# Two stages of the first expert put back to back, and its w1/w2 products in plain float32

## The chip, the cores and the metric

The kernel runs on one core of a Trainium2 chip. The core has five engines with a queue of instructions each: TensorE (PE; its weight loads are listed as PEld), VectorE (DVE), ScalarE (ACT), GpSimd (POOL) and SyncE (SP), which issues transfers. They run beside each other and wait for one another by semaphores. The metric is the time of one execution on the device in microseconds (us); the median of three runs is compared.

## The reference, cut to what matters

Three things follow one another: attention with a threshold per row, a router that sends each of 2304 tokens to one of eight experts with 288 places each, and a gated network that is the same for all tokens.

```python
scores = np.matmul(q, k.transpose(0, 1, 3, 2)) / np.sqrt(64)      # 4 x 8 heads, 576 x 576
thresh = scores.max(axis=-1, keepdims=True) - tau
x = softmax(np.where(scores >= thresh, scores, -1e9)) @ v          # -> 2304 x 512

order = np.argsort(-(x @ w_gate_router).flatten())                 # 2304 x 8 logits, best first
for idx in order:                                                  # greedy, at most 288 per expert
    tok, e = idx // 8, idx % 8
    if assigned[tok] < 0 and counts[e] < 288:
        assigned[tok] = e; counts[e] += 1

for e in range(8):                                                 # 512 -> 1024 -> 512
    y[assigned == e] = np.maximum(x[assigned == e] @ w1[e], 0) @ w2[e]

gate = 1 / (1 + np.exp(-(y @ w_gate)))                             # 512 -> 1536
out = (gate * (y @ w_val)) @ w_out                                 # 1536 -> 512
```

## The kernel before, in words

**Attention** takes the first part of the span, up to about 390 us, with its orders written out by hand in tables. It leaves the tokens `xd` in device memory and the logits.

**The router** (`Router`, lines 593 to 899) works in eight rounds. Each round searches a threshold, by counting on VectorE and small products on TensorE (line 682: up to 18 passes with 8 columns; line 700: one pass that carries the found bits to all partitions), picks one expert with its 288 tokens and writes their numbers as `idx` (TensorE: lines 830 to 832 and the 18 passes of line 864). The first rounds use `search`, those from `WIDE` = 3 on `search_wide`, which reloads tiles `kw`. A round's first steps need nothing of the expert products. Its expert is done in the order in which the rounds find it, so "first expert" is that of round 0.

**The expert part** has two stages per expert. The tokens of one expert are the 288 columns of every product.

- `arrive(e)`: POOL gathers the tokens by `idx` (three transfers), TensorE turns them (line 1183, twelve transposes in four groups), ScalarE writes the high part `xh` and VectorE the low part `xl` of the turned tokens.
- `stage_m(e)`, the w1/w2 stage: eight products `m1` with pieces of w1 and eight products `m2` with pieces of w2. All products with weights are made of parts: a float32 matrix w is split into a high part and a remainder, both in the format fp32r, and so is x, and one product is `wh*xh + wl*xh + wh*xl`, four passes of each, twelve in all (`thrice`, line 1139, and `onto`, line 1149). A pair of pieces comes as one tile `wr` of 512 KB (line 1211); ScalarE makes the high part (line 1220), VectorE the remainder with `minus` (line 1047), into the tiles `w0` and `w1`. Between `m1` and `m2` the result is passed through relu and split into `hh` and `hl`. After the eighth `m2`, ScalarE and VectorE write the sums out of four accumulators as `yh` and `yl` (line 1134).
- `stage_g(e)`, the gate/val/out stage: twelve times a gate product, a val product and, one step behind, an out product of the gated values `gh` and `gl`. Then the results are turned back into rows (line 1351), copied as `orow` (line 1358) and scattered by POOL.

The weights of gate, val and out are the same for all experts: 36 pieces. Thirteen of them are made ready during attention. The other 23 come as packed tiles `wd` of 512 KB (line 1071) and cost VectorE three narrowing steps (lines 1080 to 1086) and a `minus` each during the first experts. The out weights are stored in parts (`wod`) and loaded again as `wo` for every later expert.

**What sets the order.** `Plan` (from line 922) builds the order of all queues when the kernel is built. Every piece of work is a job with an engine, an estimated duration, the jobs it needs, a priority (a lower number goes first) and the buffers (`Hold`) it takes or uses: among them 3 tiles `wr`, 2 `w0`, 2 `w1`, 3 PSUM tiles for products and nine large tiles shared by `xh`, `xl`, `yh`, `yl`, `wd` and `kw`. `step` always places the job that can start first by the estimates. On TensorE the expert products form a row of their own, the main row: first the jobs that are ready "late enough" (by their `lag`, from `PATIENT`: 15 for the transposes, 30 for the rows), then the main row, then the rest. `open_stage` says which stage comes next in the main row. There is one special arrangement: the first two steps of the first expert's gate/val/out stage (four products) stand ahead of the second expert's w1/w2 stage, and the rest behind it. Between the last attention work and the first product, `warm` (line 1468) puts `PB` = 7 products that nobody uses.

```python
m_seq[1] = g_seq[0][:4] + m_seq[1]
g_seq[0] = g_seq[0][4:]
```

## Time and profile before

| | |
|---|---|
| median of three runs | 1159.14 us (1158.89 to 1161.96) |
| profiled execution, its own time | 1159.21 us |
| its span on the core | 1157.4 us |
| mean granted TensorE clock | 0.966 |
| TensorE busy | 92% of the span, 7938 matmul records |
| VectorE busy | 72%, 2015 instructions |
| ScalarE, GpSimd busy | 45%, 28% |

The span runs from the first to the last recorded event; 1.8 us of the execution's time lie around it. The line `PEclk` of the profile cuts the span in 40 slices of 29 us: the digit is the mean clock that TensorE was granted, in tenths of full speed. TensorE knows two levels, 1.2 and 2.4 GHz, so a clock of 0.5 in a stretch means that all of it ran at the lower one. The first product of the first expert starts at 406.4 us. The share of busy time of an engine is an average over stages that differ; the tables by stretch below tell them apart. A row of the order of time gives start, duration, engine, line, output from inputs and count, and in brackets how long the engine had stood before and what ended the wait. A row of a group gives the number of instructions, then their busy time in all and the mean duration of one in ns, then the idle time ahead of them.

### The profile page before, as it was taken

The page shows a single profiled execution, that of the slowest core. Times are in us where ns is not written, and L with a number is a line of the kernel's source. Part 1 is how long each engine was busy: PE and PEld are TensorE (multiplying, and loading weights), DVE is VectorE, ACT ScalarE, POOL GpSimd, SP SyncE. Part 2 cuts the span into 40 slices and gives each one's busy share as a digit, 9 for nine tenths or more (in the row PEclk, how much of TensorE's full clock was granted, in tenths as well). Part 3 has the DMA queues.
Part 4 walks back from the last instruction along what each step waited for, and adds up shares of the span by engine and source line. Part 5 has one row for each costly group of instructions (what it writes and reads, how often), then busy time and mean ns, then how long its engine had stood idle before and what let it go on. Part 6 is the DMA issues. An engine that isn't in the chain of part 4 may idle for free.

```text
span 1157.4 us, 21194 instructions
## 1 busy us (share of the span) xinstructions
PE 1063.9 (92%) x7938; PEld 994.1 (86%) x7938; DVE 837.1 (72%) x2015; ACT 526.2 (45%) x1120; POOL 323.0 (28%) x334
## 2 busy tenths in 40 slices
PE   4899998999995398999999999999999999999997
PEld 3787877878784297999999899999999999999996
DVE  7999999999997888988587786975973412412411
ACT  4788887788873333533214313413413413413411
POOL 6788888788841100001002001100100100000001
PEclk9999999999997597999999999999999999999998
DMA  7322423323104654454635536435544434433232
GB/s 278 141 84 94 143 84 116 121 84 131 51 18 162 210 182 166 174 191 175 194 110 163 154 107 188 148 106 161 166 118 142 151 110 132 144 110 117 71 110 92
DMA packets 52887, 156.20 MB, mean 135 GB/s; under 512 B 11568, under 2 KB 16560, under 8 KB 50864
## 3 DMA queue, kind: packets, MB, share of 16 engines
q1 hardware_dynamic: 49712, 145.40, 38.6%
q0 software_dynamic: 3072, 9.44, 2.8%
q8 instruction: 63, 1.03, 0.4%
q14 instruction: 40, 0.33, 0.1%
HBM read 135.38 MB, written 19.43 MB: 134 GB/s over the span
## 4 chain that ended last, share of the span: by engine, by line
PE 34%; DVE 30%; issue 25%; DMA 6%; ACT 2%; POOL 1%; SPq 1%; DVEq 0%; POOLq 0%; ACTq 0%
PE ps L1139 15%; PE acc L1149 9%; DVE p L281 6%; DVE nm L259 6%; PE s L248 4%; DVE big L763 3%; DVE th L267 2%; DVE lo L346 2%; PE t L289 1%; DMA kw<-kx 1%; DMA wf<-wf 1%; PE o L373 1%; PE o L365 1%; DVE w L1047 1%; POOL out L1362 1%
## 5 line engine op out<-in xcount | busy, mean ns | idle before, releaser
L1307 DVE TENSOR_TENSOR gt<-ps,sg 128x288 f32<-128x288 f32 x96 | 43.7, 455 | 146.3 <-PE ps L1139 137.2
L1362 POOL DMA_INDIRECT out<-orow,idx x24 | 23.8, 990 | 409.2 <-ACT orow L1358 406.8
L1149 PE MATMUL acc<-gh,wo 128*128 128x288 f32 x768 | 124.0, 298 | 6.0 <-DMA wo<-wod 3.0
L1303 ACT ACTIVATE sg<-ps 128x288 f32<-128x288 f32 x96 | 39.5, 411 | 196.0 <-PE ps L1139 155.3
L263 ACT ACTIVATE e<-s,nm 128x576 f32<-128x576 f32 x144 | 104.9, 741 | 37.8 <-DVE nm L259 35.5
L1047 DVE TENSOR_TENSOR w<-wr,w 128x512 fp32r<-128x512 f32 x128 | 86.3, 689 | 49.2 <-ACT w L1220 48.3
L1220 ACT ACTIVATE w<-wr 128x512 fp32r<-128x512 f32 x128 | 79.1, 629 | 90.5 <-PE acc L1149 38.3
L1311 ACT ACTIVATE gh<-gt 128x288 fp32r<-128x288 f32 x96 | 42.6, 444 | 161.4 <-DVE gt L1307 159.0
L1149 PEld LDWEIGHTS acc<-gh,wo 128*128 128x128 f32 x768 | 108.0, 188 | 7.8 <-issue 2.6
L248 PE MATMUL s<-kh,qs 128*128 128x288 f32 x320 | 80.2, 333 | 34.1 <-DVE p L281 23.4
L1139 PE MATMUL ps<-yh,wgh 128*128 128x288 f32 x384 | 108.5, 304 | 3.3 <-ACT orow L1358 2.1
L1164 POOL DMA_INDIRECT xr<-xd,idx x16 | 15.4, 960 | 337.0 <-issue 155.8
L259 DVE TENSOR_REDUCE nm<-s 128x1 f32<-128x576 f32 x144 | 104.1, 748 | 4.5 <-PE s L248 3.7
L1139 PE MATMUL ps<-yh,wvh 128*128 128x288 f32 x384 | 106.9, 300 | 0.0
L1139 PE MATMUL ps<-yh,wgl 128*128 128x288 f32 x384 | 106.7, 299 | 0.0
L1139 PE MATMUL ps<-yh,wvl 128*128 128x288 f32 x384 | 105.4, 297 | 0.0
L281 DVE SCALAR_TENSOR_TENSOR p<-s,th,e 128x576 f32<-128x576 f32 x128 | 100.1, 808 | 4.3 <-ACT tf L319 0.5
L248 PEld LDWEIGHTS s<-kh,qs 128*128 128x128 f32 x320 | 52.5, 196 | 55.2 <-issue 35.0
L1149 PE MATMUL acc<-hh,w 128*128 128x288 f32 x512 | 84.3, 299 | 0.9 <-ACT ot L1341 0.9
L1139 PE MATMUL ps<-xh,w 128*128 128x288 f32 x512 | 82.5, 304 | 0.6 <-DVE w L1047 0.3
L289 PE MATMUL t<-idf,p 128*128 128x128 f32 x548 | 80.1, 279 | 0.9 <-ACT lo L344 0.7
L763 DVE TENSOR_SCALAR_CACHE_REDUCE big<-kw,tw 128x1152 bf16<-128x1152 f32 x56 | 79.1, 1412 | 1.8
(229 smaller groups left out, 2775.0 us busy)
## 6 DMA issues: line engine op xcount, KB each, us to landing
wo<-wod SPq DMA_DIRECT2D x84, 512.0 KB
wr<-in_w SPq DMA_DIRECT2D x64, 512.0 KB
qkr<-in_qk SPq DMA_DIRECT2D x15, 1248.0 KB
wd<-in_w SPq DMA_DIRECT2D x36, 512.0 KB
wod<-wo SPq DMA_DIRECT2D x12, 512.0 KB
vr<-in_v SPq DMA_DIRECT2D x16, 320.0 KB
kw<-kx SPq DMA_DIRECT2D x64, 72.0 KB
xd<-xl SPq DMA_DIRECT2D x8, 512.0 KB
```

The costliest lines, as they stand in the source:

```text
L248: nc.tensor.matmul(s[:, h, 0:288], qs[:, qo : qo + 128], kt[:, ko + 288 * h : ko + 288 * h + 288], start=m == 0, stop=m == len(src) - 1,)
L259: nc.vector.tensor_reduce(d[u]["nm", i], d[u]["s", i][:, :, 0:288], op=OP.max, axis=AX.XY, negate=True)
L263: nc.scalar.activation(e, d[u]["s", i][:, :, 0:288], AF.Exp, bias=d[u]["nm", i])
L281: nc.vector.scalar_tensor_tensor(dst.rearrange("p (c n) -> p c n", c=2), w["s", i][:, :, 0:288], nmth[n // 2][1][:, n % 2 : n % 2 + 1], w[ ...
L289: nc.tensor.matmul(t[:m, 128 * j : 128 * j + 128], src, idf, is_transpose=True, start=j == 0, stop=j == len(srcs) - 1, skip_group_check=True,)
L763: v.tensor_scalar(self.big, self.kw[h], thr, None, op0=OP.is_ge, op1=OP.add, accum_out=cnt[:, h : h + 1])
L1047: V.tensor_sub(l, x, h.bitcast(F32))
L1139: nc.tensor.matmul(ps, w(q), x[:, q], start=n == 0, stop=n == 11)
L1149: nc.tensor.matmul(acc[m][:, :CAP], w[:, 128 * m : 128 * m + 128], x, start=first and i == 0, stop=last and i == 2)
L1220: A.activation(box[nm][:, 0], box["r"][:, i], AF.Copy)
L1307: V.tensor_tensor(box["gt"], box["v"][:, :CAP], box["sg"], op=OP.mult)
L1311: A.activation(box["h"][0], box["gt"], AF.Copy)
```

## The change

Seven things are changed, all in the plan and in the jobs of the expert part.

1. The products of the first expert's w1/w2 stage are plain float32 matmuls: four passes of 128 rows each, written once, from `wr` as it was loaded and from unsplit `xh` and `hh`. Its splits (ScalarE's high parts and VectorE's remainders, 16 of each), `xl` and `hl` fall away, and so do `w0` and `w1` for this expert; a tile `wr` is held until both its products are done.
2. The special arrangement of the main row goes. The first expert's gate/val/out stage stands whole behind its w1/w2 stage, then come the second expert's two stages.
3. What follows a product (`hh`, `hl`, the sigmoid, the gated value and its parts) gets a priority 40 below that of the stage (`NEAR`) instead of 1, `yh` and `yl` likewise; `yh` are kept in sequence, and so are the results of the out products.
4. The transposes' `PATIENT` goes from 15 to 2; those of the first expert and the rows of the last get priority -2 instead of -1, and two jobs of TensorE at -1 are kept 1.7 us apart by the estimates (`SPACE`).
5. The router's round 1 gets priority 0 instead of -5.
6. `warm` makes 18 products instead of 7.
7. Some estimates of the plan: a gather 3.8 us and 589824 bytes, SP's start at 5.5, a plain product 2.12.

Lines behind the top of the expert part move down: 1139 becomes 1144, 1149 becomes 1154, 1183 becomes 1188, 1211 becomes 1216. The plain products stand in lines 1239 (w1) and 1262 (w2).

```diff
...
+        self.free["SP"] = START
...
-                can = [(r, j) for r, j in can if r + j.lag <= self.free[e]] + main + [(r, j) for r, j in can if r + j.lag > self.free[e]]
+                late = [(r, j) for r, j in can if (r + j.lag if j.prio != -1 else max(r + j.lag, self.spaced)) <= self.free[e]]
+                can = late + main + [x for x in can if x not in late]
...
+            if j.prio == -1:
+                self.spaced = t + SPACE
...
-        hx = {e: [Hold(big), Hold(big)] for e in range(8)}
+        hx = {e: [Hold(big) for i in range(2 if e else 1)] for e in range(8)}
...
-                return 196608
+                return 589824
...
-            gathered = gather_job[e] = job("POOL", 3.2, gather, (), None, acq=hr)
+            gathered = gather_job[e] = job("POOL", 3.8, gather, (), None, acq=hr)
...
-                a = first = job("PE", 0.27, tr, [gathered] if q == 0 else [gathered, first], -1, acq=[hp_] + (hx[e] if q == 0 else []), use=hr + (hx[e] if q else []), lag=PATIENT[0] if e else 0.0)
+                a = first = job("PE", 0.27, tr, [gathered] if q == 0 else [gathered, first], -1 if e else -2, acq=[hp_] + (hx[e] if q == 0 else []), use=hr + (hx[e] if q else []), lag=PATIENT[0] if e else 0.0)
                 b = job("ACT", 0.32, evh, [a], pr, use=[hp_] + hx[e])
-                last.append(job("DVE", 0.39, evl, [b], pr, use=[hp_] + hx[e]))
+                last.append(job("DVE", 0.39, evl, [b], pr, use=[hp_] + hx[e]) if e else b)
...
-                    a = job("ACT", 0.56, hi, [ld], pr, acq=[hd], use=[hr])
-                    half.append(job("DVE", 0.64, lo, [a], pr, use=[hd, hr]))
+                    if e:
+                        a = job("ACT", 0.56, hi, [ld], pr, acq=[hd], use=[hr])
+                        half[i] = job("DVE", 0.64, lo, [a], pr, use=[hd, hr])
...
+                    if e == 0:
+                        for q in range(4):
+                            nc.tensor.matmul(
+                                box["ps"][:, :CAP], box["r"][:, 0, 128 * q : 128 * q + 128], X[0][0][:, q], start=q == 0, stop=q == 3
+                            )
+                        return
...
+                    if e == 0:
+                        for m in range(4):
+                            nc.tensor.matmul(
+                                accs["a"][m][:, :CAP], box["r"][:, 1, 128 * m : 128 * m + 128], box["h"][0], start=j == 0, stop=j == 7
+                            )
+                        return
...
-                a = job("PE", 1.59, m1, [half[0]] + x_dep, None, acq=[hps], use=[h0] + hx[e])
-                b = job("ACT", 0.32, evh, [a], base - 1, acq=[hh], use=[hps])
-                b = job("DVE", 0.39, evl, [b], base - 1, use=[hps, hh])
-                c = job("PE", 1.59, m2, [b, half[1]], None, acq=[hacc] if j == 0 else [], use=[h1, hh] + ([hacc] if j else []))
+                own = [h0] if e else [hr]
+                a = job("PE", 1.59 if e else 2.12, m1, [half[0]] + x_dep, None, acq=[hps], use=own + hx[e])
+                b = job("ACT", 0.32, evh, [a], base - NEAR, acq=[hh], use=[hps])
+                if e:
+                    b = job("DVE", 0.39, evl, [b], base - NEAR, use=[hps, hh])
+                own = [h1] if e else [hr]
+                c = job("PE", 1.59 if e else 2.12, m2, [b, half[1]], None, acq=[hacc] if j == 0 else [], use=own + [hh] + ([hacc] if j else []))
...
-                pr = pos_m[e] + 15
+                pr = pos_m[e] + 16 - NEAR
...
+                a.order = yhi[:1]
...
-                s = job("ACT", 0.31, sig, [a], base - 1, acq=[hsg], use=[hpg])
+                s = job("ACT", 0.31, sig, [a], base - NEAR, acq=[hsg], use=[hpg])
...
+                od[-1].order = od[:1] if m else []
...
-        m_seq[1] = g_seq[0][:4] + m_seq[1]
-        g_seq[0] = g_seq[0][4:]
...
-            if m < 8 and (m == g or m - g < 2 and (m == 1 or xl_jobs[m][-1].end is not None and all(d.end is not None for j in m_seq[m][:2] for d in j.deps))):
+            if m < 8 and (m == g or m - g < 2 and xl_jobs[m][-1].end is not None and all(d.end is not None for j in m_seq[m][:2] for d in j.deps)):
...
-                        job("PE", 2.5, warm, [prev], -1, acq=[Hold(pw)])
+                        job("PE", 5.5, warm, [prev], -1, acq=[Hold(pw)])
...
-            j = job(eng, dur, fn, deps, -1000 if r == 0 else -5 if r == 1 else pos_m[r] - (12 if r == 2 else AHEAD), acq=acq, use=use)
+            j = job(eng, dur, fn, deps, -1000 if r == 0 else 0 if r == 1 else pos_m[r] - (12 if r == 2 else AHEAD), acq=acq, use=use)
...
-PATIENT = 15.0, 30.0
-WD, NWF, LEAD, LATE, PB, WIDE, AHEAD = 4, 3, 14, 3, 7, 3, 40
+NEAR = 40
+PATIENT = 2.0, 30.0
+START, SPACE = 5.5, 1.7
+WD, NWF, LEAD, LATE, PB, WIDE, AHEAD = 4, 3, 14, 3, 18, 3, 40
...
```

How the order of the instructions moves, at three places. Numbers behind an underscore in a name are those of a buffer.

TensorE, the end of the first expert's w1/w2 stage. `hh` and `hl` are the parts behind relu, line 830 to 832 and 864 the last steps of round 1, `yh`/`wgh`/`wgl` the first gate product. Before:

```order
L1149 MATMUL acc<-hh,w_5871 128x288 x2
L1149 MATMUL acc<-hl,w_5871 128x288
L830 LDWEIGHTS tri
L830 MATMUL rps<-s,tri 128x1
...
L832 LDWEIGHTS one
L832 MATMUL rps<-s,one 128x1
L864 LDWEIGHTS oh_5998
L864 MATMUL rps<-rh,oh_5998 96x6
...
L864 MATMUL rps<-rh,big 96x6
L1139 MATMUL ps<-yh,wgh 128x288
```

After:

```order
L1262 MATMUL acc<-hh,wr 128x288 x4
L830 LDWEIGHTS tri
L830 MATMUL rps<-s,tri 128x1
...
L832 MATMUL rps<-s,one 128x1
L1262 MATMUL acc<-hh,wr 128x288 x4
L1144 MATMUL ps<-yh,wgh 128x288
...
L1144 MATMUL ps<-yl,wvh 128x288 x4
L864 LDWEIGHTS oh_5875
L864 MATMUL rps<-rh,oh_5875 96x6
```

Line 864 of round 1 moves from ahead of the first gate product to behind the first val product, and the count of lines 830 to 832 to ahead of the last product of w2.

TensorE, the transposes of the second expert (`idf` is the unit matrix, `xr` and `xs` the gathered rows). Before:

```order
L1139 MATMUL ps<-yl,wvh 128x288 x4
L1183 MATMUL ps<-idf,xr 128x96 x2
L1183 MATMUL ps<-idf,xs 128x96
...
L1139 MATMUL ps<-xh,w_6006 128x288 x8
L1139 MATMUL ps<-xl,w_6006 128x288 x4
```

After:

```order
L1144 MATMUL ps<-yl,wvh 128x288 x4
L700 LDWEIGHTS one
L700 MATMUL rps<-fl,one 128x8
L1188 MATMUL ps<-idf,xr 128x96 x2
L1188 MATMUL ps<-idf,xs 128x96
...
L1154 MATMUL acc<-gh,wo 128x288 x8
L1154 MATMUL acc<-gl,wo 128x288 x4
L1144 MATMUL ps<-yh,wgh 128x288
```

All four groups stood behind the second val product of the first expert and directly ahead of the second expert's first product. Now three of them stand in the middle of the first expert's gate/val/out stage; the fourth stands at that stage's end, ahead of the second expert's first product.

SP, the loads during the first expert's w1/w2 stage, with the semaphores that each waits for (`wr` is a tile of w1 and w2, `wd` a packed piece of the gate, val or out weights). Before:

```order
L1211 ISA
L1211 DMA wr<-in_w 128x1024 [waits DMAHW6_49,DMAHW2_49,DVE_49]
L1211 ISA
L1211 DMA wr<-in_w 128x1024 [waits DMAHW7_49,DMAHW3_49,DVE_49]
L1071 DMA wd<-in_w 128x1024 [waits DMASW1_49,DMASW0_49,PE_49]
L1211 ISA
L1211 DMA wr<-in_w 128x1024 [waits DMAHW0_49,DVE_49]
```

After:

```order
L1216 ISA
L1216 DMA wr<-in_w 128x1024 [waits DMAHW2_49,PE_49]
L1076 DMA wd<-in_w 128x1024 [waits DMAHW3_49,DMASW1_49,DMASW0_49]
L1076 DMA wd<-in_w 128x1024 [waits DMAHW4_49,DMASW2_49]
L1216 ISA
L1216 DMA wr<-in_w 128x1024 [waits DMAHW5_49,PE_49]
L1076 DMA wd<-in_w 128x1024 [waits DMAHW6_49]
L1076 DMA wd<-in_w 128x1024 [waits DMAHW7_49]
```

A load of `wr` waited for VectorE, the last to read the tile; now it waits for TensorE, and two loads of `wd` stand between two of `wr`.

## Rows read from the trace of the kernel before

**Rows 1.** The page: busy time of each engine, and TensorE's clock in 40 slices.

```profile
PE 1063.9 (92%) x7938; PEld 994.1 (86%) x7938; DVE 837.1 (72%) x2015; ACT 526.2 (45%) x1120; POOL 323.0 (28%) x334
...
PEclk9999999999997597999999999999999999999998
```

**Rows 2.** Busy time by stretch: us, busy time per engine, clock, DMA share, GB/s.

```profile
404.00:410.50 6.50, 6.24 (x42) 5.71 (x41) 5.75 (x16) 1.99 (x6) 0.00 (x0) 0.50 0.49 165
410.50:439.20 28.70, 28.70 (x273) 26.79 (x273) 25.49 (x75) 12.45 (x26) 0.00 (x0) 1.00 0.41 146
442.00:448.50 6.50, 5.99 (x36) 5.82 (x37) 5.76 (x18) 3.05 (x5) 1.02 (x2) 0.53 0.78 284
455.00:462.00 7.00, 6.53 (x29) 5.97 (x30) 5.64 (x12) 3.53 (x8) 0.00 (x0) 0.51 0.45 163
489.00:493.00 4.00, 4.00 (x20) 3.71 (x19) 3.26 (x9) 0.48 (x1) 0.00 (x0) 0.57 0.40 135
1004.50:1008.00 3.50, 3.50 (x17) 3.50 (x16) 0.12 (x1) 0.41 (x1) 0.76 (x2) 0.51 0.44 155
493.00:610.00 117.00, 114.63 (x928) 111.10 (x927) 89.02 (x235) 31.34 (x69) 5.56 (x9) 1.00 0.52 167
610.00:1000.00 390.00, 381.64 (x2936) 375.17 (x2935) 249.46 (x653) 126.67 (x284) 30.31 (x45) 1.00 0.47 144
```

**Rows 3.** TensorE's order of time around the first expert, 397 to 458.

```profile
397.66 3.02 PE L1468 MATMUL ps<-big,tri 128*128 128x512 bf16 x7
...
406.44 2.26 PE L1139 MATMUL ps<-xh,w 128*128 128x288 f32 x8 [0.26 <-PE rps L700]
...
442.46 1.31 PE L864 MATMUL rps<-rh,oh 128*96 128x6 bf16 x12 [3.04 <-DVE rh L857]
...
455.37 0.42 PE L1183 MATMUL ps<-idf,xr 96*128 96x96 f32 x1 [1.70 <-DMA xr<-xd,idx]
...
457.75 2.29 PE L1139 MATMUL ps<-xh,w 128*128 128x288 f32 x8
```

**Rows 4.** TensorE: a group by line and form, then the order of time.

```profile
L389 PE MATMUL o<-r,ot 128*128 128x72 f32 x248 | 31.8, 272 | 0.1
...
44.44 1.01 PE L389 MATMUL o<-r,ot 128*128 128x72 f32 x8
45.29 0.60 PE L289 MATMUL t<-idf,pt 128*128 128x128 f32 x4
...
82.02 1.03 PE L289 MATMUL t<-idf,p 128*128 128x128 f32 x8
82.81 0.47 PE L361 MATMUL o<-hi,vh 128*128 128x512 f32 x1
...
1131.48 0.30 PE L1139 MATMUL ps<-yh,wgh 128*128 128x288 f32 x1
...
1136.21 0.30 PE L1139 MATMUL ps<-yh,wgh 128*128 128x288 f32 x1
```

**Rows 5.** Groups by line: whole span; line 682 from 406.5 to 439.

```profile
L1047 DVE TENSOR_TENSOR w<-wr,w 128x512 fp32r<-128x512 f32 x128 | 86.3, 689 | 49.2 <-ACT w L1220 48.3
...
L1134 DVE TENSOR_TENSOR yl<-acc,yh 128x288 fp32r<-128x288 f32 x32 | 12.5, 450 | 1.5 <-ACT yh L1128 1.5
...
L682 PE MATMUL rps<-C,big 128*31 128x8 bf16 x54 | 1.8, 167 | 0.0
```

**Rows 6.** The order of time: a load of `wr` issued, and its first use.

```profile
469.85 0.34 SPq L1211 DMA_DIRECT2D wr<-in_w  x1
...
473.25 0.63 ACT L1220 ACTIVATE w<-wr 128x512 fp32r<-128x512 f32 x1 [0.22 <-DMA wr<-in_w]
```

**Rows 7.** TensorE's order of time: waits behind the first expert.

```profile
487.17 2.02 PE L1149 MATMUL acc<-gh,wo 128*128 128x288 f32 x8 [0.98 <-DVE yl L1134]
...
571.68 1.30 PE L1149 MATMUL acc<-gh,wo 128*128 128x288 f32 x8 [1.59 <-DMA wo<-wod]
...
1004.03 0.40 PE L1139 MATMUL ps<-yh,wgh 128*128 128x288 f32 x1 [2.06 <-ACT orow L1358]
```

## What the change does to the time: the prediction

> **What bounds the kernel now.** I read the page first: TensorE is busy for 92% of the span, VectorE for 72%, and the granted clock is at full level nearly everywhere behind the attention part [rows 1]. From 400 us on TensorE is the engine that everything waits for, so a change is worth what it does to TensorE's own work, to the gaps in its row and to its clock. The table by stretch shows where that is lost [rows 2]: from 410.5 to 439.2 it is busy without a gap at full clock, and VectorE beside it for 25.5 of 28.7 us; four short stretches (from 404, 442, 455 and 489 us) have a granted clock of 0.50 to 0.57, which is the lower of its two levels (1.2 of 2.4 GHz) for most of each. The order of time on TensorE gives the reasons [rows 3]. It stands for 3.04 us up to 442.46 for VectorE's `rh`, and then for gathered rows of the second expert, 1.70 us up to 455.37 alone, until that expert's first product starts at 457.75. Each time it stands or does little first, and then the clock is found at half. So between 439.3 and 457.8, 18.5 us, it does four products, one router step and one set of transposes.
>
> **The products without parts.** At full clock three products of split parts take 1136.21 less 1131.48, 4.73 us, or 1.58 each, 0.131 for each of twelve passes [rows 4]. Sixteen of them go: 25.2 us. In their place stand 64 plain float32 products of 288 columns. The trace has no such product. The plain float32 products of line 389 show that one is executed as two records, each with a load: 248 records (8 more stand under another name) for 16 times 8 products. Lower bound: each record at the price of a split pass, 0.26 us a product, 17 us in all, a gain of 8. Upper bound: eight records of 72 columns at line 389 take 0.85 us (44.44 to 45.29), 0.106 each; were all of that streaming, 288 columns would cost 0.43 a record and 0.85 a product, 54 us, a loss of 29. The nearest row is float32 of 128 columns, the transposes of line 289: eight from 82.02 to 82.81, 0.099 each, so 0.22 for 288 columns, 0.45 a product. I take 0.49, a little to the upper side: 31.4 us, **+6.2**.
>
> The Trainium skill (FP8 and Floating Point Precision, TensorE Precision Notes) says that true FP32 is four passes through the array. By that and the 0.131 us of a pass a product would take 0.53, the term would be +8.4 and the sum 1154.9; the two records of line 389 neither show nor exclude it.
>
> **The start.** The first product starts at 406.44 and runs at half clock until 410.5: 4.06 us, half of them lost, 2.0 [rows 2, 3]. The warm-up grows from 7 products, which take 3.02 us at half clock, to 18; the eleven more at full clock, 0.2 each, carry it from 400.7 to about 403. Between it and the first product there remain a search step and the transposes, which need the gathered rows, so the first product itself starts as before (it no longer waits for `xl`, but a search step now stands ahead of the transposes). Whether the clock lasts over this is open: between nothing and 2.0 I take half, **-1.0**.
>
> A rule speaks against this term: the Trainium skill (TensorE: Matmul & The Clock Gate, Part 4, PE-mode transpose) says that transposes don't count as busy for the clock. The trace agrees as far as it goes, half clock from 404 on with TensorE busy for 6.24 of 6.5 us of mostly transposes, searches and the first products. By the rule the term is 0 and the sum 1153.7.
>
> **From 439 to 458.** The 18.5 us hold four products (6.3), the router step of line 864 (1.3) and the transposes (1.6 of the 2.4 that they take from 455.37 on at half clock): 9.2, so 9.3 were lost [rows 3]. The change moves line 864 behind the first gate and val product, and three of the second expert's four groups of transposes into the middle of the gate/val/out stage, some 15 us behind the indices; the gather takes about 9 (442.5 plus the step, to 455.8). Both waits go. What is late next is `y`: after the last product ScalarE must evacuate four `yh` and VectorE four `yl` of 0.45 us each [rows 5], behind some 4.5 us of router and weight work in VectorE's queue, while TensorE has 2.1 us of product and 1.1 of gate that need no `yl`. I put 2.0 of standing and half a fall of the clock, 1.0: 3.0. **-6.3**.
>
> **The first stage's covers.** Two things are costed nearly at nothing. VectorE loses 16 splits of w1/w2 at 86.3/128 = 0.67 us [rows 5] and takes gate/val/out weights and the router in their place; by my count it then has 7.1 us of work for each search step against TensorE's two or four products and search of about 5 to 7. And a tile `wr` is now held until its second product is done, so the next load is issued only then: it lands in 3.4 us (issued 469.85, used at 473.25) [rows 6], against two products (3.9) and a search (54 passes for three of them take 1.8, so 0.6 [rows 5]), 4.5 us, until it is needed. SP's queue puts `wd` loads of the same 512 KB between them, and the last seven of these behind five `wr` of the second expert; they feed out weights that are needed only late in the next stage, and cost nothing. POOL's gathers and scatters keep their sequence. **+1.5** for both, between 0 and the price of the slower rival below.
>
> **What follows from the order.** The second expert's stage no longer begins at half clock: 457.75 to 461.9 at the lower level, **-2.0**. The handover at 487 (0.98 us of waiting for `yl`, a group of 2.02 us that takes 1.2 elsewhere, and 3.4 us at half clock: 3.5 in all) [rows 2, 7] becomes one between other stages; I expect 2.0 of it to stay, **-1.5**. The waits for `wo` around 571 (1.59) [rows 7] had the router's `kw` transfers beside them; these move into the w1/w2 stage, **-1.4**. The gate/val/out stage now follows without the 25 us in which weights could be got ready. In 493 to 610 VectorE had 89 us of work in 117 and TensorE nearly no gap [rows 2]; in the new stage I count about 51 us on VectorE against 58 on TensorE, so only single periods run over, **+1.0**. From 610 to 1000 there are 8.4 us of gaps, and at 1004 there are 2.06 for `orow` and 1.7 lost to half clock [rows 2, 7]. Evacuations there get precedence in the plan (`NEAR`), but an engine doesn't stop what it has begun, and `rows` still take the three PSUM slots ahead of gate: I take a quarter of 12.1, **-3.0**. The end (rows, scatter) stands as it was: 0.
>
> **Sum.** 6.2 - 1.0 - 6.3 + 1.5 - 2.0 - 1.5 - 1.4 + 1.0 - 3.0 = -6.5. The profiled execution took 1159.21 us (span 1157.4), which is the median of the runs shown to within 0.1: 1159.2 - 6.5 = **1152.7**.
>
> **Rivals.** *A, the weights come too late (slower).* In the first stage five tiles `wr` are loaded just in time. With two `wd` (1 MB) ahead, at the 284 GB/s of the stretch from 442 [rows 2] 3.6 us, a load would land at 7.0 instead of 3.4, 2.5 beyond its cover: 12.5 us for the five, and two falls of the clock at 1.7, less the 1.5 counted: 1152.7 + 14.4 = 1167.1. It decides from a landing of about 6.2 us on. Against it: mean traffic in 410 to 439 is 146 GB/s, and no wait for `wr` shows on TensorE in the stage as it is. Chance 0.12.
>
> *B, the waits come back elsewhere (no change).* VectorE, which loses the spread over two stages, is late for `yl` and for the searches: the handover costs 6 instead of 3, the one at 487 keeps its 3.5 (+1.5), and behind 610 nothing is gained (+3.0): 1152.7 + 7.5 = 1160.2. For it: VectorE busy for 25.5 of 28.7 us in the stage as it is. Chance 0.24.
>
> *C, the small waits go too.* The covers hold (-1.5), the handovers are short (-3.0), the start is warm (-1.0): 1147.2. Chance 0.16.
>
> *D, the plain product is cheap*, at the lower bound: 1152.7 - 14.5 = 1138. Nothing but the two records speaks for it. Chance 0.05.
>
> That the change doesn't move what it says is excluded by the order of the instructions.
>
> **How the numbers follow.** The forecast, with 1150 to 1156 around it, has 0.43. A measurement of this kernel tells a change from none from about 0.3% on, 3.5 us: faster is below 1155.7, slower above 1162.6. Faster: 0.39 of the forecast, C and D, 0.60. Same: 0.04 of the forecast, 0.20 of B, 0.02 of A: 0.26. Slower: 0.10 of A and 0.04 of B: 0.14. The range reaches from C's lower side, 1146, to B's upper side, 1162; left out are D and most of A, about 0.16. By their sign the cases below 1155.7 have their own range, 1146 to 1155.7.
>
> **What would show it.** In the profile after: 64 products of 288 columns in 128 records, 0.24 us apart (0.13 or 0.43 would be the bounds); the first stage 36 us long, with TensorE busy throughout and no wait for `wr`; no wait for `xr` ahead of the second expert, whose first product follows an out product at full clock; a gap of about 2 us ahead of the first gate. The forecast is wrong if TensorE waits for `wr` or for `fl` in the first stage, if a gate product waits for its weights, or if a half-clock stretch stands behind the first stage as long as those at 442 and 455.

## The result, and the profile after

The changed kernel takes 1146.45 us (median of four runs, 1144.91 to 1150.95), the kernel before 1159.02 beside it: a ratio of 0.9896 with a 95% interval of 0.9871 to 0.9921. A second set of five runs gave 1148.01, ratio 0.9901 (0.9882 to 0.9919). The change is faster by 10.4 to 12.6 us. The forecast was 1152.7, faster by 6.4, with a range down to 1146.

The page of the changed kernel's profile, busy time of each engine and the granted clock in 40 slices, against [rows 1]. This execution was the longest of the four (span 1149.2).

```profile
PE 1068.4 (93%) x7884; PEld 990.7 (86%) x7885; DVE 819.8 (71%) x1987; ACT 517.6 (45%) x1104; POOL 323.9 (28%) x334
...
PEclk9999999899998599999899999999999999999999
```

A slice is 28.7 us here, 28.9 before. The sixteenth, from 434 us on before and at 0.7, is at full clock (from 431 us on); a new 0.8 stands in the one from 546 us; the 0.5 is the slice of the first search, in both. The 0.8 at 201 us lies in attention. VectorE has 17 us less to do. The table by stretch (columns as in [rows 2]), from a second profile of the same order of instructions (span 1146.6): the first expert's w1/w2 stage, its gate/val/out stage, the second expert's w1/w2 stage.

```profile
406.30:444.70 38.40, 36.86 (x229) 26.75 (x227) 36.64 (x101) 11.32 (x23) 0.00 (x0) 1.00 0.74 254
444.70:511.50 66.80, 66.46 (x571) 62.52 (x569) 57.32 (x159) 22.87 (x47) 2.91 (x3) 1.00 0.51 175
511.50:548.50 37.00, 31.64 (x248) 30.33 (x246) 27.11 (x69) 17.82 (x39) 4.98 (x8) 0.98 0.67 196
```

In the first stage VectorE is now busy for 36.64 of 38.40 us, as long as TensorE. The second has TensorE busy without a gap; before, this stage was cut in two, with the second expert's w1/w2 stage between. In the third TensorE stands for 5.4 of 37 us: the new loss.

TensorE's order of time in the first profile, plain products (a group of eight records is one product with four blocks of 128 rows) and the handover to the first gate product:

```profile
425.69 2.21 PE L1239 MATMUL ps<-xh,wr 128*128 128x288 f32 x8
427.74 2.10 PE L1262 MATMUL acc<-hh,wr 128*128 128x288 f32 x8
429.77 0.61 PE L682 MATMUL rps<-C,big 128*31 128x8 bf16 x18
...
443.61 2.19 PE L1262 MATMUL acc<-hh,wr 128*128 128x288 f32 x8
445.42 0.51 PE L1144 MATMUL ps<-yh,wgh 128*128 128x288 f32 x1
```

A group takes 427.74 - 425.69 = 2.05 us, 0.51 for a block of 128 rows. The first gate product follows the last plain one with no wait, where [rows 3] had 3.04 us for `rh`.

The new loss, in the order of time of the second profile. SP issues:

```profile
530.00 9.08 SPq L748 DMA_DIRECT2D kw<-kx  x16
539.33 8.08 SPq L1216 DMA_DIRECT2D wr<-in_w  x5
```

ScalarE behind it:

```profile
543.09 1.15 ACT L1225 ACTIVATE w<-wr 128x512 fp32r<-128x512 f32 x2 [4.25 <-DMA wr<-in_w]
...
546.14 1.29 ACT L1133 ACTIVATE yh<-acc 128x288 fp32r<-128x288 f32 x4
...
547.88 0.62 ACT L1382 ACTIVATE orow<-ps 96x512 f32<-96x512 f32 x1
```

And TensorE:

```profile
548.56 0.61 PE L1144 MATMUL ps<-yh,wgh 128*128 128x288 f32 x1 [2.84 <-ACT orow L1382]
```

SP issues sixteen transfers of the router's `kw` for 9.08 us; the `wr` loads of the third expert come behind them; ScalarE stands 4.25 us for one, with `yh` of the second expert and `orow` of the first queued behind that; the gate product waits 2.84 us for `orow` and starts at half clock (0.50 up to 553, 1.00 from 554 us on). The first profile has the same wait with 3.34 us, so it belongs to the order.

### The profile page after: what moved, and what is told of

Its sections match the earlier page's. It is cut to its first block, busy times and chain, and to the rows that moved or that the text cites. A ratio compares the mean times of both kernels' runs of the same rounds, so it can differ in the third digit from the quotient of the medians.

```text
span 1149.2 us, 21045 instructions
## 1 busy us (share of the span) xinstructions
PE 1068.4 (93%) x7884; PEld 990.7 (86%) x7885; DVE 819.8 (71%) x1987; ACT 517.6 (45%) x1104; POOL 323.9 (28%) x334
## 4 chain that ended last, share of the span: by engine, by line
PE 40%; issue 26%; DVE 25%; DMA 4%; ACT 2%; POOL 2%; SPq 0%; DVEq 0%; POOLq 0%; ACTq 0%
PE ps L1144 18%; PE acc L1154 11%; DVE nm L259 6%; DVE p L281 6%; PE s L248 4%; DVE th L267 3%; DVE lo L346 2%; PE t L289 2%; DMA wr<-in_w 1%; PE o L365 1%; DMA wf<-wf 1%; PE o L373 1%; DVE wf L1088 1%; POOL out L1386 1%; DMA wd<-in_w 1%
## 5 line engine op out<-in xcount | busy, mean ns | idle before, releaser
L1052 DVE TENSOR_TENSOR w<-wr,w 128x512 fp32r<-128x512 f32 x112 | 75.6, 689 | 54.7 <-ACT w L1225 53.8
L1225 ACT ACTIVATE w<-wr 128x512 fp32r<-128x512 f32 x112 | 69.2, 629 | 75.8 <-PE acc L1154 31.9
L1144 PEld LDWEIGHTS ps<-yh,wgh 128*128 128x128 f32 x384 | 72.8, 189 | 8.7 <-ACT orow L1382 4.9
L289 PEld LDWEIGHTS t<-idf,p 128*128 128x128 f32 x548 | 66.0, 145 | 14.0 <-ACT tf L319 2.2
```

The costliest lines, as they stand in the source:

```text
L289: nc.tensor.matmul(t[:m, 128 * j : 128 * j + 128], src, idf, is_transpose=True, start=j == 0, stop=j == len(srcs) - 1, skip_group_check=True,)
L1052: V.tensor_sub(l, x, h.bitcast(F32))
L1144: nc.tensor.matmul(ps, w(q), x[:, q], start=n == 0, stop=n == 11)
L1225: A.activation(box[nm][:, 0], box["r"][:, i], AF.Copy)
```

## The experiments

Each kernel is the changed one with one thing altered, unless it says otherwise. Times of the stages are read from the order of time of one profiled execution, from first product to first product. "Start" is the first expert's first product; "first two" is the sum of the four stages of the first two experts (the kernel before and e2 have other stages there); "last part" runs from the third expert's first product to the last expert's first gate product. Behind that every profile has 67.4 us more, so start, first two, last part and 67.4 make its span. A profiled execution can lie some us off its kernel's median. e8 to e10 and e11 ran on two other chips than e1 to e7; the median of the kernel before was between 1157.7 and 1158.8 us beside each of them.

| kernel | median us | start | first w1/w2 | first gate | second w1/w2 | second gate | first two | last part |
|---|---|---|---|---|---|---|---|---|
| before | 1158.4 | 406.4 | | | | | 208.3 | 475.3 |
| changed, second profile | 1148.0 | 406.3 | 38.4 | 66.8 | 37.1 | 61.4 | 203.6 | 469.3 |
| e1 parts | 1157.0 | 404.5 | 32.1 | 74.8 | 32.6 | 60.2 | 199.7 | 479.5 |
| e2 old order | 1162.9 | 405.1 | | | | | 215.4 | 471.9 |
| e3 NEAR 1 | 1149.7 | 402.4 | 41.2 | 72.1 | 34.0 | 58.2 | 205.5 | 473.7 |
| e4 warm-up 7 | 1146.0 | 402.8 | 37.2 | 66.7 | 38.1 | 61.7 | 203.7 | 469.4 |
| e5 order alone | 1161.0 | 406.2 | 38.1 | 72.3 | 31.1 | 65.0 | 206.5 | 477.7 |
| e6 one transfer | 1157.0 | 408.6 | 38.1 | 65.9 | 38.3 | 60.5 | 202.8 | 477.6 |
| e7 parts, one transfer | 1166.0 | 404.2 | 32.1 | 74.8 | 32.6 | 66.3 | 205.8 | 487.2 |
| e8 parts, no remainders | 1149.1 | 410.6 | 32.6 | 64.6 | 32.9 | 62.7 | 192.7 | 477.8 |
| e9 parts, GpSimd | 1157.3 | 412.9 | 41.1 | 64.5 | 29.9 | 62.9 | 198.4 | 478.0 |
| e10 kw in the plan | 1148.1 | 404.9 | 38.5 | 65.9 | 32.6 | 62.2 | 199.2 | 474.2 |
| e11 twice | 1162.1 | 409.4 | 44.1 | 74.3 | 39.6 | 60.5 | 218.5 | 471.2 |

**The changed kernel again.** One number is put back, with no effect on the order of any engine:

```diff
-... 0 if r == 1 else ...
+... -5 if r == 1 else ...
```

> The changed kernel with the priority of the router's round 1 put back from 0 to -5; the order of instructions is the same on every engine, so this is the changed kernel a second time. Its profiled execution took 1150.95 us, 4.5 more than the median of its runs, and shows TensorE waiting 3.34 us up to 551 and at half clock for 6.8 us there. If that wait is an accident of transfers in one execution, a second profile is without it and its span is about 6 us shorter (1143); if it belongs to the order, it stands there again and the shorter runs gain elsewhere. Median expected: 1146.4.

1148.01 us. The wait up to 548.56 stands there again: order, not accident. The priority of round 1 does nothing here.

**Parts again.** The hunks of the diff that make the first expert's products plain are undone.

> The changed kernel with the first expert's w1/w2 products in split parts again, all else as changed. Forecast's theory: TensorE's own work counts in full, 33.0 us of plain products become some 26, and VectorE's extra splits (16 of 0.69 and 12 remainders of 0.45, 16.5 us) are put off into the stage behind: 1146.4 - 7 + 1 = 1140. Rival: the plain products pay for themselves, since VectorE was busy for 36.1 of 37.4 us of that stage: with 16.5 us more, the gate/val/out weights come late, gaps of 6 to 12 us stand in the first expert's gate/val/out stage, and the time is 1146 to 1152.

1157.03 (ratio to before 0.9987, 0.9971 to 1.0003): of the gain nearly nothing is left, and the forecast's theory, by which the splits put off onto VectorE cost 1 us, has fallen. The two stretches of the first expert:

```profile
404.40:436.50 32.10, 32.10 (x290) 30.30 (x288) 29.41 (x75) 14.15 (x28) 0.00 (x0) 0.95 0.47 165
436.50:511.30 74.80, 66.49 (x493) 63.67 (x494) 69.08 (x169) 27.45 (x55) 3.26 (x4) 0.93 0.62 216
```

The waits of TensorE in the second, by what was waited for (us in total, times, longest):

```profile
PE acc L1154 <- DVE wo L1052: 4.0, 3, 1.7
PE acc L1154 <- ACT wo L1108: 3.0, 2, 2.2
```

The w1/w2 stage wins 6.3 us, as forecast for TensorE's work, and the next gives 8.0 back: VectorE is busy 69.08 of 74.8 us and the out weights are late. So the first expert's stages together lose 1.7 us by the parts. The second expert's two are 5.7 us shorter than in the changed kernel, without the wait up to 548.56, and the start is 1.9 earlier; the rest of this execution's loss stands in the last part, 10.2 us. The profiled execution was the fastest of its twelve; 4 us of the median are in no profile.

**The old order of stages.** The two lines on `m_seq[1]` and `g_seq[0]` and the case `m == 1` are put back.

> The changed kernel with the old order of stages (two steps of the first expert's gate/val/out stage, then the second expert's w1/w2 stage). Forecast's theory: the gather of the second expert stands open again, since only two products of 1.6 us and a search step stand between the router's last step and the transposes, against some 9 us for the gather: 4 to 6 us of waiting and a fall of the clock of 3.4, 1146.4 + 8 = 1154. Rival: with the router's step moved ahead the wait is gone whatever the order, and the time is 1146 to 1148.

1162.91 (1.0042, 1.0025 to 1.0059), slower than before. TensorE's order of time behind the second val product:

```profile
459.59 1.30 PE L682 MATMUL rps<-C,big 128*63 128x8 bf16 x18 [5.95 <-DVE big L637]
```

The granted clock is 0.53 from 456 to 470 us. The wait at the joint comes back: the second val product starts at 451.81, the second expert's first product at 467.46. But the waits that the trace names there are 7.7 us for VectorE's search and 0.4 for the gathered rows, which end a wait only at 462.48. The price came, nearly twice the one expected; that the gather sets it, as the theory has it, holds at most for the part behind the search.

**The old precedence.**

```diff
-NEAR = 40
+NEAR = 1
```

> The changed kernel with NEAR at 1, the old precedence of what follows a product. If the small waits behind 612 us (9.0 us of gaps before, 4.4 after) went because of NEAR, some 5 of them come back: 1151. If they went because transposes and rows stand elsewhere, the time stays at 1146 to 1148. At NEAR 1 the router's last step of round 1 moves ahead of the first gate product again, which by the forecast's theory costs another 1.5 to 3: 1148 at least.

1149.71 (0.9918, 0.9903 to 0.9932), 1.7 above the changed kernel. Line 864 of round 1 stands ahead of the first gate product again, as expected, and TensorE waits 1.2 us there, 0.73 of it for `rh`. The last part takes 4.4 us longer, of the 6.0 that the change won there. TensorE's waits there, with NEAR 1:

```profile
PE ps L1144 <- ACT orow L1382: 4.1, 3, 1.5
PE ps L1144 <- DVE yl L1139: 1.8, 1, 1.8
```

and in the changed kernel:

```profile
PE ps L1144 <- DVE yl L1139: 1.8, 1, 1.8
PE ps L1144 <- ACT orow L1382: 1.1, 1, 1.1
```

**The short warm-up.** `PB` is 7, the estimate of `warm` 2.5.

> The changed kernel with 7 warm-up products instead of 18; the order of all other instructions is the same. Forecast's theory: the longer warm-up lets the first product find full clock in part of the executions, worth 1 to 2 us: 1149. Rival: transposes and search steps stand between the warm-up and the first product, the clock falls whatever came before, and the time stays at 1146 to 1148.

1145.99 (0.9898, 0.9879 to 0.9916), the same as with 18. The first products run at 0.58 of the clock here (402.7 to 404.5), at 1.00 in the changed kernel's second profile and at half in its first; but the first product also comes sooner here, 8.4 us behind the start of the warm-up, against 9.2 and 10.9.

**The order alone, on the kernel before.** The same two lines are taken out of the kernel before; products in parts, old precedence.

> The kernel before with the order of stages alone changed (the first expert's gate/val/out stage whole behind its w1/w2 stage; products in parts, old precedences). Forecast's theory: the wait for the gathered rows goes and nothing else: 1158.4 - 7 = 1151. Rival, by which the order needs the plain products: VectorE has the splits of w1 and w2 and the gate/val/out weights on hand at once, TensorE waits for out weights some 8 us in the stage, and the time is 1156 to 1160.

1161.01 (1.0034, 1.0019 to 1.0048): slower than before. The wait for the gathered rows is gone, as the theory says, and the first two experts take 1.8 us less than before; but the last part takes 2.4 more, and the gain of 7 doesn't come. The handover keeps its wait,

```profile
442.47 0.64 PE L864 MATMUL rps<-rh,oh 128*96 128x6 bf16 x6 [3.03 <-DVE rh L857]
```

since line 864 stays ahead of the first gate product, and the gate/val/out stage takes 72.3 us, 4.7 of it waits for `gh`, where the rival had waits for out weights. In e3 line 864 stands at the same place and the wait for `rh` is 0.73: with plain products the old precedence alone doesn't bring the 3.03 back.

**One transfer for half a kw.**

```diff
-            for e in range(8):
-                nc.sync.dma_start(
-                    self.kw[h][16 * e : 16 * e + 16],
-                    self.kx[e : e + 1, 64 * h : 64 * h + 64].rearrange("a p c -> a (p c)").to_broadcast([16, T // 2]),
-                )
+            nc.sync.dma_start(
+                self.kw[h],
+                self.kx[:, 64 * h : 64 * h + 64].rearrange("a p c -> a (p c)").unsqueeze(1).to_broadcast([8, 16, T // 2]),
+            )
```

> The changed kernel with the router's tiles kw loaded by one transfer each instead of eight, same bytes, same plan. In the second profile of the changed kernel SP issues sixteen of them from 530.0 to 539.1 us, and the next loads of wr only then; ScalarE then stands 3.7 us for wr ahead of orow and yh, and TensorE 2.84 us up to 548.56, with half clock behind it. If SP's issuing is the cause, the wait goes and the clock stays: 1147.5 - 5 = 1142.5. If the bytes are the cause (1.2 MB at some 250 GB/s, 4.7 us), the wait stays and the time is 1146 to 1148.

1156.98 (0.9986, 0.9967 to 1.0006), 9 us slower than the changed kernel, which neither of the two expectations had. SP is free after 1.44 us, but the data come later. The issue on SP, in the order of time:

```profile
530.59 1.44 SPq L747 DMA_DIRECT2D kw<-kx  x2
```

The first use of the second half on VectorE:

```profile
544.54 1.41 DVE L762 TENSOR_SCALAR_CACHE_REDUCE big<-kw,cf 128x1152 bf16<-128x1152 f32 x1 [3.54 <-DMA kw<-kx]
```

And ScalarE's wait for the next load of `wr`, which SP now issues at 534.68:

```profile
545.40 1.15 ACT L1224 ACTIVATE w<-wr 128x512 fp32r<-128x512 f32 x2 [5.45 <-DMA wr<-in_w]
```

The second half is ready 12.5 us after both were issued, VectorE stands 3.54 us, ScalarE 5.45 instead of 4.25, and the gate product still waits 2.56. So SP's issuing alone is not the cause. The single transfer has another shape, too (eight rows of sixteen copies, where each of the eight has sixteen copies of one row), and no run tells the number of transfers from the shape. The loss itself stands in the last part, 8.3 us, where `kw` is loaded for the later rounds and TensorE waits 3.4 us for `rhw`; the first two experts take 0.8 less.

**Parts and one transfer.** Both edits together.

> The changed kernel with the first expert's products in parts and kw loaded by one transfer each. If the loss of the parts (1157.0 against 1148.0) lay in VectorE's work alone, it stays at about 9 beside the kernel with plain products and the same kw; the part of it that came from late loads at the later handovers goes here too. By the stages of the profile with parts I expect 8 us of loss in the first expert's gate/val/out stage against 6.3 won in its w1/w2 stage, so 2 more than the plain kernel with the same kw (1144 to 1145) if the rest is an accident of the order, and 1151 to 1153 if it is not.

1166.01 (1.0077, 1.0052 to 1.0101), 9.0 above the kernel with plain products and the same `kw`, as e1 is above the changed one. The first expert's stages repeat e1's; the last part takes 487.2 us. The expected 2 was wrong: the part of e1's loss that lies in the last part stayed.

**Parts without the remainders.** The sixteen `minus` of the first expert's w1 and w2 are left out; the products read the high part twice.

> The changed kernel with the first expert's products in parts, and the sixteen remainders of its w1 and w2 left out on VectorE (the products read the high part in their place, so TensorE does the same twelve passes): that part of the computation is missing. It takes 11 us off VectorE and nothing off TensorE. If VectorE's work is why the parts lose (1157.0 against 1148.0), the stages of the first expert come out at 32 and 67 us (32.1 and 74.8 with the remainders, 38.4 and 66.8 with plain products) and the time is 1141 to 1146. If the parts lose because the orders of the later stages differ, the first expert gains little and the time stays at 1153 or above.

1149.09 (0.9906, 0.9877 to 0.9936). The two stages of the first expert:

```profile
410.60:443.20 32.60, 32.60 (x289) 30.78 (x288) 30.01 (x77) 16.47 (x32) 0.00 (x0) 0.94 0.49 178
443.20:507.80 64.60, 63.02 (x532) 60.91 (x531) 61.88 (x162) 24.75 (x51) 2.80 (x3) 1.00 0.61 213
```

32.6 and 64.6: with 11 us off VectorE and the same work on TensorE, the 74.8 us of the parts become 64.6. VectorE is the reason for the loss in that stage. The last part is 8.5 us longer than in the changed kernel all the same, though VectorE has no more to do in the first expert than there (91.9 us in the two stages, 94.0 there): that loss is another one. The start is 4.3 us later in this execution, 2.28 of it a wait for gathered rows.

**Parts, remainders on GpSimd.**

> The changed kernel with the first expert's products in parts and the sixteen remainders of w1 and w2 made by GpSimd, which does nothing in that stage and takes 1.3 us for a remainder of this shape in attention (48 of them, 62.6 us). 21 us of work for 32 us of stage. By the theory that VectorE is the reason: 1141 to 1146, as with the remainders left out. Rival: GpSimd's results come too late for TensorE (1.3 us against 0.69 each, two for 3.2 us of products) or slow VectorE beside it, and waits of 0.5 us or more stand ahead of most products of the stage: 1150 to 1157.

1157.25 (0.9994, 0.9979 to 1.0008); the rival was right on VectorE, but its waits ahead of most products didn't come. The w1/w2 stage takes 41.1 us instead of 32.1, and not for GpSimd's results but for VectorE's search; the longest wait of TensorE:

```profile
427.92 0.16 PE L700 MATMUL rps<-fl,one 31*128 31x8 bf16 x1 [3.42 <-DVE fl L695]
```

VectorE in order of time:

```profile
417.18 0.46 DVE L1137 SCALAR_TENSOR_TENSOR hl<-ps,hh 128x288 fp32r<-128x288 f32 x1 [1.04 <-ACT hh L1133]
...
421.59 1.76 DVE L1088 SCALAR_TENSOR_TENSOR wf<-wd,wf 128x512 int32<-128x512 int32 x1
423.39 1.66 DVE L1091 SCALAR_TENSOR_TENSOR wf<-wd,wf 128x512 int32<-128x512 int32 x1
424.96 0.41 DVE L1085 TENSOR_SCALAR wf<-wd 128x512 int32<-128x512 int32 x1
425.41 0.69 DVE L1088 SCALAR_TENSOR_TENSOR wf<-wd,wf 128x512 int32<-128x512 int32 x1
...
426.39 1.19 DVE L717 SCALAR_TENSOR_TENSOR w<-n,w 128x1 int32<-128x1 int32 x1
...
442.40 1.52 DVE L1085 TENSOR_SCALAR wf<-wd 128x512 int32<-128x512 int32 x1
```

GpSimd beside it:

```profile
416.92 1.29 POOL L1231 TENSOR_TENSOR w<-wr,w 128x512 fp32r<-128x512 f32 x1 [13.19 <-ACT w L1225]
...
421.36 1.45 POOL L1231 TENSOR_TENSOR w<-wr,w 128x512 fp32r<-128x512 f32 x1 [0.75 <-ACT w L1225]
423.00 1.49 POOL L1231 TENSOR_TENSOR w<-wr,w 128x512 fp32r<-128x512 f32 x1 [0.20 <-ACT w L1225]
426.30 1.26 POOL L1231 TENSOR_TENSOR w<-wr,w 128x512 fp32r<-128x512 f32 x1 [1.81 <-ACT w L1225]
...
442.36 2.72 POOL L1231 TENSOR_TENSOR w<-wr,w 128x512 fp32r<-128x512 f32 x2 [1.82 <-ACT w L1225]
```

A narrowing step of 0.69 us takes 1.66 and 1.76 when it begins while one of GpSimd's subtractions runs, and a step of the search on one column, 0.15 elsewhere in the stage, takes 1.19. The start is 6.6 us later than in the changed kernel's second profile, with a wait of 3.00 us for VectorE in the first search, and the last part is 8.7 longer; the four stages between are 5.2 shorter.

**kw in the plan.**

```diff
-            yield "SP", 2.7, "kw2" if h else "kw"
+            yield "SP", 4.7, "kw2" if h else "kw"
```

> The changed kernel with the plan's estimate for issuing the eight transfers of half a kw raised from 2.7 to 4.7 us (the sixteen take 9.1 to 9.9 us in the profiles). The plan then expects the next loads of wr later, and puts yh and orow of the second expert ahead of the splits that wait for them on ScalarE. If that standing order is why TensorE waits 2.84 us up to 548.56 and runs at half clock behind it, both go: 1147 - 5 = 1142. If the transfers themselves hold up more than ScalarE's queue, the wait moves and the time is 1146 to 1149.

1148.09 (0.9912, 0.9887 to 0.9937). At its place the theory holds. ScalarE now has `yh` and `orow` ahead of the next splits that wait for `wr`,

```profile
539.95 1.29 ACT L1133 ACTIVATE yh<-acc 128x288 fp32r<-128x288 f32 x4
541.19 1.57 ACT L1382 ACTIVATE orow<-ps 96x512 f32<-96x512 f32 x3
543.60 1.16 ACT L1225 ACTIVATE w<-wr 128x512 fp32r<-128x512 f32 x2 [0.85 <-DMA wr<-in_w]
```

the second expert's w1/w2 stage takes 32.6 us instead of 37.1 and the gate product behind it waits for nothing. The plan also puts one load of `wr` between the two halves of `kw`, at 534.53; which of the two moves does it, this run doesn't tell. The 4.5 us are given back: the last part takes 4.9 more, with a new wait ahead of the third expert's gate products:

```profile
635.41 0.17 PE L769 MATMUL rps<-rhw,one 128*128 128x8 bf16 x1 [2.28 <-DVE rhw L766]
```

**The remainders of gate, val and out twice.**

```diff
-                minus(l, box["f"].rearrange("p (k f) -> p k f", k=4), h)
+                for i in range(2 if n >= pre else 1): minus(l, box["f"].rearrange("p (k f) -> p k f", k=4), h)
```

> The changed kernel with the remainder of each of the 23 gate/val/out pieces that come as wd computed twice on VectorE, the plan and the order of all else untouched: 15.9 us more of VectorE (23 of 0.69), about what the split products of the first expert would add (16.5), and nothing on TensorE. VectorE was busy 36.6 of 38.4 us and 57.3 of 66.8 us in the first expert's two stages, 11.3 us of slack. If VectorE's work sets the loss of the split products, waits for line 1052 and for the search stand on TensorE in these stages, 6 to 10 us with the clock: 1147 + 8 = 1155, and the later stages stay as they are. If the loss was an accident of later orders, TensorE's stages get longer by 0 to 3 us: 1147 to 1150.

1162.10 (1.0033, 1.0014 to 1.0052): 14 us above the changed kernel for 15.9 us of VectorE, with the order of all else unchanged, where 8 were expected. TensorE's waits in the first expert's two stages:

```profile
PE rps L700 <- DVE fl L695: 6.3, 5, 2.4
PE ps L1144 <- DVE yl L1139: 1.3, 1, 1.3
```

The stages grow by 5.7 and 7.5 us, at a granted clock of 0.91 and 0.95, and the last part stays within 2. The profiled execution was the slowest of its twelve, 1168.2, so these two sizes are on the high side. By the median VectorE's work counts nearly in full in the changed kernel, and the waits show the way: through the search, whose short steps wait in VectorE's queue.

## Why the prediction was right, and where it was not

The time lies in the range and moved the way that was forecast, but the gain is nearly twice the 6.5 of the sum, and 1146.45 lies 0.45 above the range's lower end: with the second set at 1148.0 and e4 at 1146.0, on which side of that end a median falls is luck. By the forecast's terms:

- **What bounds the kernel**: right. TensorE's gaps and clock between 439 and 458 us were to be won, and were.
- **The plain product**: 0.51 us against the 0.49 taken, 64 make 32.8 instead of 31.4, so the term is +7.6 instead of +6.2. The Trainium skill (FP8 and Floating Point Precision, TensorE Precision Notes) gives four passes for true FP32; by the pass of 0.131 that is an estimate of 0.53 and a term of +8.4, and the trace is nearer to that than to the 0.45 of the nearest row.
- **The start**, -1.0: nothing by e4. The clock at the first product differs between executions of one order, and what it gives, the longer warm-up costs.
- **439 to 458**, -6.3: right, and a little short. No wait at the first gate, 0.8 us at the first `yl` group where 3.0 were left, no half clock. But the text gave this to the move of the instructions alone. In e5 the order takes away the wait for the gathered rows and leaves the one for `rh`, 3.03 us; in e3, with plain products and line 864 at the same place, 0.73 of it is left. So most of that wait goes without the precedence; that it goes by the plain products is likely, but no run shows it alone. e2 shows the other side: without the order the rest of the change is slower than before.
- **The covers**, "costed nearly at nothing": the size was right (the stage took 37.4 and 38.4 us for 36), the reading was not. VectorE's cover has no reserve (36.64 of 38.40), and what makes it enough is that the plain products take 16.5 us off VectorE. The forecast named the splits that go, but gave them no gain, and counted the plain products as a pure cost. e1 and e8 show what it is worth, 8 us in the first gate/val/out stage, and e11 that VectorE's work counts there. Against TensorE's 6.3 the plain products are 1.7 us to the good in the first expert. The other 7 of the 9 us that e1 loses lie behind it and aren't explained by this.
- **The handover behind the second expert's w1/w2 stage**, 2.0 to stay: 2.84 and 3.34 us of waiting and half clock behind it, 5.5 to 6 in all. This is the step that failed. **The waits for `wo`**, -1.4: they went, as said, because the `kw` transfers moved into the w1/w2 stage; but the text followed them no further, to the `wr` loads and ScalarE's queue there. In e10, where that order is another, the wait is gone.
- **The first gate/val/out stage**, +1.0: 0.3 (66.46 of 66.80 busy), though the work in it was counted too low, 51 and 58 us for VectorE and TensorE against 57.3 and 66.5. **The second expert's start**: full clock, as said.
- **Behind 610 us**, -3.0: mis-sized by half. The last part went from 475.3 to 469.3 us. TensorE's waits for `orow`, `gh`, `ot` and `wo` in it shrank or went; e3 puts 4.4 of the 6.0 on `NEAR`. Some of it is only work that stands earlier now: before, the fourth of the router's rounds (round 3) ended at 618.1, behind the third expert's first product.

All terms but the last add up to -3.5 for the way to the third expert's first product; counted from the start of the warm-up, the second profile shows 203.6 + 9.2 against 208.3 + 8.8, -4.3, the first -1.7. The rest of the miss is the last part. Rival A didn't come: the longest wait for `wr` in the first stage was 0.7 us. The measured time is that of rival C (1147.2), but not by its terms: the start gave nothing and one handover got longer.

**What stays open**: why the last part takes some 478 us or more in e1, e5, e8 and e9, and 469 to 474 in the changed kernel, e2, e3, e4, e10 and e11 (in e6 and e7 `kw` is loaded in another way). The rows show single waits at handovers (2.58 us for `xl` and 3.06 for `orow` in e1), e8 shows that VectorE's load in the first expert is not the whole reason, and e11 that the changed order keeps its 471 under that load. One thing goes with it in every profile. In the changed kernel the router's round 3 ends ahead of the third expert's first product (609.92), in e1 behind it (604.12):

```profile
596.66 0.67 PE L864 MATMUL rps<-rh,oh 128*96 128x6 bf16 x12
```

```profile
625.24 0.66 PE L864 MATMUL rps<-rh,oh 128*96 128x6 bf16 x12
```

It ends behind it in the kernel before (475.3), e1, e5, e8 and e9, where VectorE has 273 to 281 us of work in the last part, and ahead of it in the changed kernel, e2, e3, e4, e10 and e11, with 263 to 267. So a longer last part has a piece of the search in it that stands earlier elsewhere. No run moves that round by itself, so that it is the cause isn't shown. No kernel here clearly beats the changed one.

## What to carry to other kernels

An edit that looks like a price on the busiest engine may pay by what it takes off the second (here 6.3 us of price and 8.0 of relief in two stages): before the undoing of such a part is called a gain, count the second engine's busy time in the stage where its work is put off to. Parts of a change don't add up: undone one at a time, order, plain products and precedence cost 15, 9 and 2 us, of a gain of 11. A shorter stage can also mean that its work now stands in a later one, so compare the work in both. When a transfer moves to another stage, follow the queue that it is issued on to the next load, and that load to the engine that waits for it with other work queued behind.

## What the runs showed of the hardware

- A plain float32 product of 128 rows and 288 columns takes 0.51 us at full clock, in two records: 3.9 times the 0.131 of a pass of the parts.
- GpSimd's subtraction of 128x512 (1.3 to 1.8 us) held VectorE's steps up in e9. In the first expert's w1/w2 stage those that began while one ran and read only SBUF took 0.68 to 1.76 us instead of 0.15 to 0.69 and ended 0.02 to 0.55 us behind a subtraction's end; those that began ahead of it (line 1088 at 438.72, 0.69) or read PSUM (line 1137, 0.45 to 0.46) kept their time. The Trainium skill (GPSIMD Engine Reference, Key points) names contention of the two with VectorE instructions of a two-port mode or with two inputs in SBUF. Line 1088 has two such inputs, line 1137 one, and there the trace agrees; line 1085 has one and was held up too (0.41 to 1.52), and in which mode it ran no row shows.
- Eight transfers of 72 KB with a repeated source were ready sooner than one of 576 KB, though SP needs 4 to 5 us to issue them: from the first issue of both halves to VectorE's use of the second it was 11.4 us with sixteen transfers (530.00 to 541.43, second profile) and 13.9 with two (530.59 to 544.54), both times with VectorE waiting for the data. The two differ in shape as well as in number.
